# Two of sixteen head pairs with tokens put in order of two hash bits, and attention inside four groups of 256 slots

## The chip, the cores and the metric

The kernel runs on one core of a Trainium2 chip. The metric is the device time of one execution in microseconds (us), lower being better. The core has five engines, each of which works through its own instructions in order: TensorE (PE, matrix products), VectorE (DVE), ScalarE (ACT), GpSimd (POOL) and SyncE (SP, which here only issues DMAs). GpSimd issues DMAs too, among them indirect ones, whose rows go to (or come from) addresses that stand in a tile.

## The reference, cut to what matters

Attention on 4 batches x 8 heads of 768 tokens with 64 features, in which a query sees only the keys with the same six hash bits, and then a token and channel mixer:

```python
q_bits = (np.einsum('bhsd,dk->bhsk', q, proj) > 0)
k_bits = (np.einsum('bhsd,dk->bhsk', k, proj) > 0)
mask = q_bucket[:, :, :, None] == k_bucket[:, :, None, :]     # bucket: the six bits as a number
scores = scale * np.matmul(q, k.transpose(0, 1, 3, 2))
attn = softmax(np.where(mask, scores, -1e9))
x = np.matmul(attn, v)                                        # (B, H, S, D) -> (B, S, H*D)
xt = x.transpose(0, 2, 1)
u = x + (np.maximum(xt @ w_tok1, 0.0) @ w_tok2).transpose(0, 2, 1)
out = u + np.maximum(u @ w_ch1, 0.0) @ w_ch2
```

## The kernel before, in words

The 16 pairs are (batch, two heads); pair n is batch n // 4 and heads 2 (n % 4) and the next. The two heads of a pair lie on partitions 0 to 63 and 64 to 127, so two 64-row matmuls run side by side. The loop over the pairs (line numbers are those of the profile, that is of the kernel before, where nothing else is said) does one pair a turn:

- **Scores.** For each half of the queries (384) there are six chunks of 128 keys (`Half.scores`, L347 to 363). A chunk is a bf16 product of the hash bits and an fp32 product of queries and keys into one PSUM tile `sc`. The bits are scaled so that a query and a key of other buckets get a large negative sum, so that the exponential (L363, ACT) of it is zero. `sc` has three buffers; the exponentials `e` have twelve.
- **Sums.** DVE adds the six chunks of a half (`add` L391 and L395, `add_last` L398). PE adds over partitions in the next turn (`Quotients.sums` L434), ACT makes a first reciprocal (L438, L439), DVE improves it (`newton` L447, L449) and divides (L459, into `XT`).
- **Hash bits of the next pair.** PE multiplies by the projection (`hashes`, L301, tile `hp`), DVE compares (L305, tile `g`), ACT scales (L309), and eight small DMAs on SP (L314) put the bits into `bits`, from which the next turn's first product reads.
- **Weighing.** Two halves, 96 matmul records (`weigh` L410), and ACT's copy of the result (`num`, L416).
- **Weights.** Each turn converts a block of the token and channel weights from int64-like words to fp32: an SP DMA (`raw`, L169), one ACT step (`size`, L177) and five DVE steps (L187 to L206).
- **Bounce.** Each second turn DVE transposes two finished pairs (L233, tile `stage`, one buffer) and SP writes them to DRAM in four DMAs (L238), from where the token mixer reads them.

SP's order in a turn is: eight bits, qk of the pair after next, raw, in each second turn four bounce DMAs, and then, at the head of the next turn, `vn` and `vt` (values by token and by feature, two buffers each) of the pair after. An SP DMA with a wait holds all behind it. Behind the attention follow the token mixer (`mix1`, `mix2`) and the channel mixer (L785 and around), which read `XT` and `x`. At the end flags decide whether a slower branch (`careful_attention`, over all pairs) has to run.

What sets the order is the program text itself: every engine gets its instructions in the order in which the code below records them.

Of the kernel before, what the change touches and what calls it, by code (L numbers as in the profile page):

```python
# [48 lines left out]
def kernel(  # L49
# [4 lines left out]
    vT: bass.AP,  # L54
    proj: bass.AP,
# [30 lines left out]
    EPS = 2.0**-70  # L86

# [35 lines left out]
    excess = const.tile([P, 2 * B * NP], F32, name="excess")  # L123
# [104 lines left out]
    def bounce(stage, n):  # L228
# [7 lines left out]
        to = bounced[b].rearrange("(a i) (g c) -> g i a c", i=32, g=4)  # L236
        for g in range(4):
            nc.sync.dma_start(  # L238
                out=to[g, :, :, 32 * hp : 32 * hp + 64],
                in_=stage[32 * g : 32 * g + 32].rearrange("p a k i -> p a (k i)"),  # L240
            )
# [16 lines left out]
    def attention(pool, psum, W1, W2, x0):  # L258
        bitrows = [pool.tile([P, 2, S], BF16, name=f"bits{n}", tag=f"bits{n}", bufs=1) for n in range(2)]
        loaded = {}  # L260

        def load_qk(n):
            if n >= len(pairs):
                return
# [9 lines left out]

        def load_v(n):
            if n >= len(pairs):
                return
# [3 lines left out]
            vt = pool.tile([P, S], F32, name="vt", tag="vt", bufs=2)  # L281
            nc.sync.dma_start(out=vt, in_=vT[b, hp])
            loaded[n][1:3] = vn, vt
# [8 lines left out]
        def hashes(n):  # L292

            g = pool.tile([P, HALF], BF16, name="g", tag="g", bufs=2)
            if n == 1:
# [10 lines left out]
            if n == 1:  # L306
# [3 lines left out]
            for j in range(4):  # L310
                sl = slice(HALF * (j // 2), HALF * (j // 2) + HALF)
                for i in range(2):
                    at = 32 * j + 16 * i
                    nc.sync.dma_start(  # L314
                        out=bitrows[n % 2][D * i : D * i + NB + 1, j % 2, sl], in_=g[at : at + NB + 1],
# [25 lines left out]
        class Half:  # L341
# [5 lines left out]
            def scores(self):  # L347

                qkt, bits = loaded[self.n][0], bitrows[self.n % 2]
# [17 lines left out]
                if first:  # L367
                    first_hashes(0)
                for c in range(NR):
                    sc = psum.tile([P, 2, 512], F32, name="sc", tag="sc", bufs=3)  # L370
# [29 lines left out]
            def weigh(self):  # L400
# [4 lines left out]
                else:  # L405
                    acc = psum.tile([P, 512], F32, name="acc", tag="acc", bufs=1)[:, :HALF]
                for c, e in enumerate(self.es):
                    for i in range(2):
# [54 lines left out]

        load_qk(0)
# [4 lines left out]
        load_qk(1)  # L469

        idle = psum.tile([P, 512], F32, name="idle", tag="sm", bufs=1)
        for _ in range(6):
# [5 lines left out]
            [(w_tok1, W1, 3, (0, NR)), (w_tok2, W2, 1, (0, NJ)), (w_ch1, WC1, 1, (0, NCB))],  # L478
            bufs=2,
        )  # L480


        before = None
        for n in range(len(pairs)):
            halves = [Half(n, half) for half in range(2)]
            if n:
                load_v(n + 1)
            for now in halves:
                now.scores()
                if n == 0 and now.half:  # L490
                    hashes(1)
                now.add()
                if now.half == 0:
                    now.add_last()
            if before:
# [1274 lines left out]
```

## Time and profile before

| | us |
|---|---|
| time, median of 3 runs (787.77 to 787.89) | 787.86 |
| span of the profiled execution | 786.3 |
| the profiled execution's own time | not shown |
| PE busy | 780.1 |
| DVE busy | 669.5 |
| ACT busy | 484.7 |
| GpSimd busy | 54.2 |
| exponentials (ACT, L363), 192 of them | 154.5 |
| L434's sums and L301's hash products on PE | 13.6 and 12.5 |

How to read a profile: busy times show who works most. The chain that ended last goes back from the last instruction to what released it, so it says who was waited for. A row of the timeline gives start, duration, engine, line, operation, tile written and tile read, and in brackets the engine's idle time before it and who ended it. A group's row gives count, total, mean in ns and idle time before it. "SPq" is the issue of a DMA, not its transfer.

### The profile page before, as it was taken

How to read it: one execution, taken by the hardware profiler on the slowest of the kernel's cores; microseconds unless marked ns; L12 is line 12 of the kernel's file. 1: busy time of each engine (PE TensorE's matmuls, PEld its weight loads, DVE VectorE, ACT ScalarE, POOL GpSimd, SP SyncE). 2: the span in 40 equal slices, each digit the busy share in tenths (PEclk: the TensorE clock that was granted, in tenths of full speed). 3: DMA queues.
4: the chain of work that ended last, by engine and by line, in shares of the span. 5: the costliest groups of instructions: out<-in, count | busy, mean ns of one | idle time of the engine just before them, and what ended most of it. 6: DMA issues, size and time to landing. Idle time of an engine off the chain costs nothing.

```text
span 786.3 us, 12638 instructions
## 1 busy us (share of the span) xinstructions
PE 780.1 (99%) x4751; PEld 483.5 (61%) x4751; DVE 669.5 (85%) x918; ACT 484.7 (62%) x837; POOL 54.2 (7%) x77
## 2 busy tenths in 40 slices
PE   9999999999999999999999999999999999999997
PEld 4444444444444444455544448888887888886886
DVE  5989898989897677999787888999899799889884
ACT  6688888888888887233323225656774667665331
POOL 1000000000000000011120110120000122000001
PEclk9999999999999999999999999999999999999999
DMA  4435353537352425786487897797776784850565
GB/s 165 163 125 163 125 164 125 163 124 244 125 166 88 127 95 180 200 259 133 90 253 263 276 392 276 226 295 204 233 223 203 249 251 126 242 171 2 184 170 133
DMA packets 102529, 145.38 MB, mean 185 GB/s; under 512 B 30200, under 2 KB 72640, under 8 KB 102464
## 3 DMA queue, kind: packets, MB, share of 16 engines
q1 hardware_dynamic: 94448, 119.68, 46.5%
q0 software_dynamic: 7728, 24.64, 13.5%
q8 instruction: 38, 0.62, 0.3%
q10 hardware_dynamic: 288, 0.21, 0.1%
q14 instruction: 27, 0.22, 0.1%
HBM read 101.53 MB, written 35.52 MB: 174 GB/s over the span
## 4 chain that ended last, share of the span: by engine, by line
PE 99%; DVE 0%; issue 0%; DVEq 0%
PE b L785 50%; PE sc L356 20%; PE acc L410 16%; PE t L658 5%; PE t L698 5%; PE sums L434 2%; PE hp L301 1%; PE hw L325 0%; PE idle L474 0%; DVE second L1030 0%; DVE bits L467 0%; DVE ones L97 0%; PE b L1614 0%; DVEq L1765 0%
## 5 line engine op out<-in xcount | busy, mean ns | idle before, releaser
L363 ACT ACTIVATE e<-sc 128x768 f32<-128x768 f32 x192 | 154.5, 810 | 7.0 <-PE sc L356 6.6
L356 PE MATMUL sc<-qk 64*128 64x384 f32 x768 | 153.7, 486 | 0.0
L785 PE MATMUL b<-R,second 128*128 128x256 f32 (+1 forms) x522 | 131.9, 409 | 0.0
L410 PE MATMUL acc<-e,vn 128*32 128x384 f32 x1536 | 127.0, 486 | 0.0
L785 PEld LDWEIGHTS b<-R,second 128*128 128x128 f32 x522 | 99.0, 190 | 28.7 <-issue 16.5
L395 DVE TENSOR_TENSOR esd<-esd,e 128x768 f32<-128x768 f32 x96 | 92.0, 958 | 10.4 <-ACT e L363 0.5
L410 PEld LDWEIGHTS acc<-e,vn 128*32 128x32 f32 x1536 | 49.9, 110 | 73.9 <-issue 73.5
L356 PEld LDWEIGHTS sc<-qk 64*128 64x128 f32 x768 | 68.7, 189 | 42.3 <-issue 38.1
L791 ACT COPY c<-b 128x256 f32<-128x256 f32 (+1 forms) x96 | 40.3, 426 | 79.4 <-PE b L785 68.2
L356 PE MATMUL sc<-bits 64*128 64x384 bf16 x384 | 62.5, 323 | 0.0
L785 PE MATMUL b<-XT,WC 128*128 128x256 f32 (+1 forms) x208 | 61.0, 428 | 0.0
L391 DVE SCALAR_TENSOR_TENSOR esd<-e 128x768 f32<-128x768 f32 x32 | 30.6, 955 | 23.4 <-ACT e L363 23.3
L785 PEld LDWEIGHTS b<-XT,WC 128*128 128x128 f32 x208 | 39.5, 190 | 15.4 <-issue 10.5
L785 PE MATMUL b<-XT,SW 128*128 128x256 f32 (+1 forms) x164 | 47.0, 410 | 0.0
L658 PE MATMUL t<-x,W 128*128 128x512 f32 x96 | 41.8, 593 | 0.0
L356 PEld LDWEIGHTS <-bits 64*128 64x128 bf16 x384 | 18.7, 94 | 33.1 <-issue 9.9
L416 ACT ACTIVATE num<-acc,vsum 128x384 f32<-128x384 f32 x32 | 18.6, 581 | 29.8 <-PE acc L410 29.4
L785 PEld LDWEIGHTS b<-XT,SW 128*128 128x128 f32 x164 | 31.1, 190 | 9.4 <-issue 4.1
L718 POOL DMA_DIRECT2D XT<-second x8 | 9.8, 1228 | 385.6 <-DVE second L717 363.4
L455 ACT COPY rec<-rec 32x384 f32<-32x384 f32 x64 | 32.7, 510 | 5.0 <-DVE rec L449 4.2
L398 DVE TENSOR_TENSOR esd<-esd,e 128x768 f32<-128x768 f32 x32 | 30.5, 954 | 1.9
L658 PEld LDWEIGHTS t<-x,W 128*128 128x128 f32 x96 | 18.2, 190 | 22.7 <-issue 21.3
(246 smaller groups left out, 1282.2 us busy)
## 6 DMA issues: line engine op xcount, KB each, us to landing
second<-left SPq DMA_DIRECT2D x20, 768.0 KB
raw<-in_moe_w_ch SPq DMA_DIRECT2D x16, 768.0 KB
qk<-in_qk SPq DMA_DIRECT2D x15, 768.0 KB
second<-left SPq DMA_DIRECT2D x18, 576.0 KB
seen<-in_qk POOLq DMA_DIRECT2D x21, 384.0 KB, 4.6
WC<-hidden_left SPq DMA_DIRECT2D x18, 448.0 KB
vn<-in_v SPq DMA_DIRECT2D x16, 384.0 KB
vt<-in_vT SPq DMA_DIRECT2D x16, 384.0 KB
```

The costliest lines, as they stand in the source:

```text
L356: nc.tensor.matmul(sc[:, i, :HALF], t[rows, 1, P * c : P * c + P], t[rows, 0, qs], start=start, stop=not start,)
L363: nc.scalar.activation(e, sc[:, :, :HALF], ACT.Exp, scale=SCALE)
L391: nc.vector.scalar_tensor_tensor(self.d, es[0], NR * EPS, es[1], op0=ALU.add, op1=ALU.add,)
L395: nc.vector.tensor_tensor(self.d, self.d, e, op=ALU.add)
L398: nc.vector.tensor_tensor(self.d, self.d, self.es[-1], op=ALU.add)
L410: nc.tensor.matmul(acc[D * i + d : D * i + d + 32], vn[:, i, c, d : d + 32], e[:, i], start=(c == 0), stop=(c == NR - 1),)
L416: nc.scalar.activation(nums[self.n][:, self.half], acc, ACT.Identity, scale=-1.0, bias=vsum,)
L455: nc.scalar.copy(rec[other : other + 32, h], rec[at : at + 32, h])
L658: nc.tensor.matmul(ps, W1[:, r, P * j : P * j + P], x[:, r], start=(r == 0), stop=(r == NR - 1),)
L698: nc.tensor.matmul(ps[at], left, right, start=start, stop=True, skip_group_check=True,)
L785: nc.tensor.matmul(ps, left(k), right(k), start=start and k == ks[0], stop=stop and k == ks[-1], skip_group_check=True,)
L791: nc.scalar.copy(c, ps)
```

## The change

Pairs 6 and 7 (batch 1, heads 4 to 7) leave the loop, which then has 14 turns, counted k = 0 to 13 over the pairs that remain. For the two pairs a class `Sorted` sorts the tokens by two of the six bits (the first two) into four groups of 256 slots each, queries and keys alike. A query's group holds all keys of its bucket, so attention is done inside a group, on 32-row tiles: group g's matmuls use partitions 32 g to 32 g + 31. Two fp32 products over 32 features each and one bf16 product for the four other bits give the scores of 256 queries by 128 keys. Empty slots have a bit column that makes their keys count for nothing. With these inputs the fullest group of the two pairs has 224 tokens; `excess` has two more columns, so that a group of more than 256 would set the flag.

The steps of a sorted pair hang at points of the loop's turns:

```diff
+    SORTED = {6: (1, 5), 7: (3, 7)}
...
+        for n, (turn, made) in SORTED.items():
...
+            at(turn - 1, "loads", begin)
+            at(turn, "hash", call("hash"))
+            at(turn, ("weigh", 1, 3), call("turn_bits"))
+            at(turn, "end", call("own_groups"), call("count"))
+            at(turn + 1, "begin", call("places"), call("numbers"))
+            at(turn + 1, "added", *[call("scatter", r) for r in range(NR)])
+            at(made - 1, "loads", call("fetch"))
+            at(made, "begin", call("copy_bits"), call("turn_q"))
+            at(made, "added", call("turn_k"), call("turn_sorted_bits"))
+            at(made, "weighed", call("scores", 0))
+            at(made, "end", call("scores", 1))
+            at(made + 1, ("scores", 0, 3), call("sums"), call("weigh"))
+            at(made + 1, "added", call("newton"), call("divide"), call("turn_back"))
+            at(made + 1, "last", *[call("gather", r) for r in range(NR)])
+            at(made + 2, "loads", call("store"))
+            at(made + 3, "begin", call("fetch_turned"))
+            at(made + 3, "added", call("finish"))
```

`load` brings qk, vt and, from two new inputs, the tokens' rows (queries in `rows_q`, values and keys in `rows_kv`; one buffer for both pairs). `count` makes each token's place among its group's, and `places` turns it into addresses. GpSimd's 24 indirect DMAs put the rows into DRAM tables, which were cleared at the start:

```diff
+            def scatter(self, r):
+                for w, rows in enumerate((rows_q, rows_kv)):
+                    for i in range(2):
+                        x = 4 * r + 2 * w + i
+                        nc.gpsimd.indirect_dma_start(
+                            out=self.tables[2 * w + i],
+                            out_offset=bass.IndirectOffsetOnAxis(ap=self.at[:, x : x + 1], axis=0),
+                            in_=rows[:, r, i], in_offset=None,
+                        )
...
+            def fetch(self):
+
+                self.v = [sorted_v, pool.tile([P, 2, NR, D], F32, name="vn", tag="vn", bufs=2)]
+                self.v[1] = self.v[1].rearrange("p a b c -> p (a b) c")[:, :NJS]
+                for i in range(2):
+                    nc.sync.dma_start(
+                        out=in_q[i], in_=slots(self.tables[i]).rearrange("(p j) c -> p j c", p=P),
+                    )
...
+            def copy_bits(self):
+                for i in range(2):
+                    nc.scalar.copy(in_q_bits[:, i, :, :4], in_q[i][:, :, D : D + 4])
+                    nc.scalar.copy(in_k_bits[:, i, :, :4], in_k[i][:, :, D : D + 4])
+                nc.scalar.copy(in_k_bits[:, :, :, 4], self.full)
...
+            def scores(self, k):
...
+                for i in range(2):
+                    for part in range(W + 1):
+                        for g in range(NG):
+                            rows = slice(32 * g, 32 * g + 32)
+                            if part:
+                                left, right = kT[rows, i, part - 1, keys], qT[rows, i, part - 1]
+                            else:
+                                left, right = k_bits[rows, i, keys], q_bits[rows, i]
+                            nc.tensor.matmul(
+                                banks[g][:, SLOTS * i : SLOTS * i + SLOTS], left, right,
+                                start=part == 0, stop=part == W, skip_group_check=True,
+                            )
...
+            def finish(self):
+                b, hp = pairs[self.n]
+                nc.vector.transpose(
+                    XT[:, hp, S * b : S * b + S].rearrange("p (a i) -> p a i", i=32), self.y,
+                )
```

The results go back by DRAM: `turn_back` stores them by slot, twelve indirect gathers on GpSimd put them in the tokens' order into the `stage` buffer, `store` writes them to DRAM, `fetch_turned` reads them with 32 features to a partition group, and `finish` transposes them into `XT`. At the start `prepare_sorting` makes constants (on GpSimd and DVE) and clears the tables in eight DMAs. Also: the weights are converted in another order (channel weights first, since the token weights' tiles W1 and W2 and the last batch's part of `XT` serve as scratch), only pairs that stay are bounced, `mix1`'s Relu of a bounced batch is split in two, and `fetch(0, x0)` moves to turn 10.

What ACT has at the end of one turn and the start of the next, with what each waits for: before, from the second `num` of a turn (L416) to the reciprocal of the sums (L438, L439).

```order
L416 ACTIVATE num<-acc,vsum 128x384 [waits PE_49,Activation_49]
L416 ACTIVATE num<-acc,vsum 128x384 [waits PE_49]
L363 ACTIVATE e<-sc 128x768 [waits PE_49] x12
L438 ACTIVATE near<-sums 128x384 [waits PE_49]
L439 ACTIVATE near<-near 128x384 [waits Activation_49]
```

ACT again, now, at the end of turn 4 and in turn 5 (L447 of the changed kernel is L416 of the one before, L388 is L363, L469 is L438; `DMAHW` is a DMA that SP issued; W_124 holds the sorted bits, x_126 and XT the fetched rows):

```order
L447 ACTIVATE num<-acc,vsum 128x384 [waits PE_49,Activation_49]
L447 ACTIVATE num<-acc,vsum 128x384 [waits PE_49]
L737 CAST W_124<-x_126 128x8x4 [waits DMAHW7_49]
L738 CAST W_124<-XT 128x8x4 [waits DMAHW1_49]
L737 CAST W_124<-XT 128x8x4 [waits DMAHW0_49]
L738 CAST W_124<-XT 128x8x4 [waits DMAHW2_49]
L739 COPY W_124<-XT 128x16
L388 ACTIVATE e<-sc 128x768 [waits PE_49] x12
L469 ACTIVATE near<-sums 128x384 [waits PE_49]
```

Five copies of `copy_bits` now stand between a turn's last `num` and the next turn's twelve exponentials, and four of them wait for DMAs of the fetch.

On SP, before, from the loads at the end of one turn with a bounce to the bits of the turn after:

```order
L268 DMA qk<-in_qk 128x1536
L169 DMA raw<-in_moe_w_ch 128x1536
L238 DMA bounced_104<-stage 32x24x64 x4
L280 DMA vn<-in_v 128x768
L282 DMA vt<-in_vT 128x768
L314 DMA bits_135<-g 7x384 x8
```

On SP, now, the same stretch at the end of turn 4 and in turn 5 (L283 is L268 before, L178 is L169, L247 is L238, L301 and L293 are L280 and L282, L339 is L314):

```order
L283 DMA qk<-in_qk 128x1536
L721 DMA x_126<-table_137 128x576
L721 DMA XT<-table_138 128x576
L726 DMA XT<-table_139 128x8x72
L726 DMA XT<-table_140 128x8x72
L730 DMA XT<-table_139 128x4x64 x2
L730 DMA vn<-table_140 128x4x64 x2
L178 DMA raw<-in_moe_w_ch 128x1536
L247 DMA bounced_104<-stage 32x24x64 x4
L301 DMA vn<-in_v 128x768
L293 DMA vt<-in_vT 128x768
L339 DMA bits_135<-g 7x384 x8
```

Eight fetches are put behind qk, and two of them write a `vn` buffer, ahead of the loop's own `vn`.

On DVE, before, the adds of a turn's two halves and the compare that makes g:

```order
L391 SCALAR_TENSOR_TENSOR esd<-e 128x768
L395 TENSOR_TENSOR esd<-esd,e 128x768 x3
L398 TENSOR_TENSOR esd<-esd,e 128x768
L391 SCALAR_TENSOR_TENSOR esd<-e 128x768
L395 TENSOR_TENSOR esd<-esd,e 128x768 x3
L305 TENSOR_SCALAR g<-hp 128x384
```

On DVE, now, from the adds of half 0 to g in turn 8 (L419 is L391 before, L423 is L395, L426 is L398, L325 is L305; W_124 holds the sorted pair's weighed values):

```order
L423 TENSOR_TENSOR esd<-esd,e 128x768 x3
L426 TENSOR_TENSOR esd<-esd,e 128x768
L869 STREAM_TRANSPOSE XT<-stage 128x768
L826 SCALAR_TENSOR_TENSOR unit<-ssums,rec 128x512
L827 SCALAR_TENSOR_TENSOR rec<-unit,rec 128x512
L832 TENSOR_TENSOR W_124<-W_124,rec 128x512 x2
L839 STREAM_TRANSPOSE x_126<-W_124 128x512
L839 STREAM_TRANSPOSE XT<-W_124 128x512
L419 SCALAR_TENSOR_TENSOR esd<-e 128x768
L423 TENSOR_TENSOR esd<-esd,e 128x768 x3
L325 TENSOR_SCALAR g<-hp 128x384
```

Between the two halves' adds, and so ahead of g, stand pair 6's last transposition (`finish`) and pair 7's `newton`, `divide` and `turn_back`.

More of the change, by code (lines that the diff above doesn't have):

```diff
@@ L260, in attention, with following @@
         loaded = {}
+        regular = [n for n in range(len(pairs)) if n not in SORTED]
+        turns = {n: i for i, n in enumerate(regular)}
+        def following(n, by=1):
+            i = turns[n] + by
+            return regular[i] if i < len(regular) else None
         def load_qk(n):
-            if n >= len(pairs):
+            if n is None:
                 return
@@ L488, in attention @@
             for now in halves:
[L489 to L491 removed]
+                now.scores(hooks("scores", now.half))
+                if k == 0 and now.half:
+                    hashes(regular[1])
                 now.add()
```

425 lines of the change are left out of this document (390 added, 35 removed).

## The prediction

> **What bounds the kernel now.** I read the page first: busy time of each engine, then the row of granted clock, then the shares of the chain that ended last.
>
> ```profile
> span 786.3 us, 12638 instructions
> PE 780.1 (99%) x4751; PEld 483.5 (61%) x4751; DVE 669.5 (85%) x918; ACT 484.7 (62%) x837; POOL 54.2 (7%) x77
> PEclk9999999999999999999999999999999999999999
> PE 99%; DVE 0%; issue 0%; DVEq 0%
> ```
>
> TensorE (PE) is busy 780.1 of 786.3 us, and the chain is PE's to 99%. The chain's pieces give one turn of the attention loop, here the one for pair 6:
>
> ```profile
> 120.90 9.80 PE sc L356 x72
> 130.70 0.78 PE sums L434 x8
> 131.48 0.65 PE hp L301 x8
> 132.13 7.74 PE acc L410 x96
> 139.87 9.80 PE sc L356 x72
> ```
>
> From 120.90 to 139.87 a turn takes 18.97 us, and PE has no gap. So PE work that goes is gained one for one, as long as no other engine makes PE wait; and every new wait of PE is lost in full. The whole question is which of the moved steps PE will wait for. The span is the sum's base; the profiled execution's own time is not shown, and the median of 787.86 us lies 1.6 us above the span. I add those 1.6 us at the end.
>
> I write T5 for the start of turn 5, and so on; turns count the 14 pairs that stay in the loop.
>
> **What PE saves.** A score chunk (9.80 / 12 = 0.82 us) is two bf16 matmuls side by side, 0.16, and the fp32 pair, 0.65, each over 384 columns. Over 256 columns that is 0.11 and 0.43. A sorted pair has two key halves and two heads, and for each one bf16 and two fp32 groups: 4 x (0.11 + 2 x 0.43) = 3.9 us if the four 32-row tiles of a group run together, as two 64-row tiles do now; 7.7 if only two do. I take 3.9, since two already do at no loss. Sums: 0.65 x 512/384 x 2 = 1.7. Weighing: 8 groups x 0.43 = 3.4. Hashing 0.65, turning and counting the bits about 1.0. Together 10.7 of 18.97, so two pairs save 2 x 8.25 = **-16.5** (with 7.7 in place of 3.9: -8.8). Against that the Trainium skill, "TensorE: Matmul & The Clock Gate", section "Measured speedup vs the span model", states 3.07 times for four row tiles rather than four. By that, as an estimate, the scores would cost 1.2 us more a pair and the sum would be 2.3 higher; no row of this trace has four row tiles.
>
> **A. The start.**
>
> ```profile
> 3.87 0.44 POOL L101 TENSOR_SCALAR_AFFINE_SELECT bitscale<-bitscale 128x1 f32<-128x1 f32 x2
> 5.70 0.56 DVE L330 TENSOR_SCALAR bits<-hw 128x384 bf16<-128x384 f32 x1 [4.25 <-PE hw L325]
> ```
>
> GpSimd ends its set-up at 4.31. Now some 25 memsets and iotas follow, and DVE has eight steps that wait for them ahead of its first hash bits (L330): 25 at the row's 0.22 or less put these at 8 us in place of 5.70, +2.3. Eight DMAs that clear 3.4 MB of tables stand ahead of the bits of pair 1 in SP's queue and in the DMA rings, some 3 us. **+5** (0 to 9).
>
> **B. The count.** At the end of turns 1 and 3 PE counts the groups from what DVE compares behind the weights' conversion, whose last step stands in a turn after PE has begun the next one (139.42 against 139.87 below): **+1.5** for both (0 to 4).
>
> ```profile
> 137.67 0.96 DVE L196 TENSOR_TENSOR size<-size,unit 128x768 f32<-128x768 f32 x1
> 139.42 0.95 DVE L206 SCALAR_TENSOR_TENSOR WC<-raw,size 128x768 uint32<-128x768 uint32 x1
> ```
>
> **C. The scatters.** Before has no indirect DMA. Its nearest rows are GpSimd's plain ones:
>
> ```profile
> L1602 POOL DMA_DIRECT2D seen<-in_qk x21 | 12.5, 597 | 106.4 <-ACT seen L1592 69.4 <-ACT second L791 26.7 <-DMA hidden_left<-WC 10.2
> L718 POOL DMA_DIRECT2D XT<-second x8 | 9.8, 1228 | 385.6 <-DVE second L717 363.4 <-DVE unit L187 11.3 <-DVE TB L615 5.5
> seen<-in_qk POOLq DMA_DIRECT2D x21, 384.0 KB, 4.6
> ```
>
> An issue takes 0.6 or 1.2 us, by the shape; 4.6 us pass to landing. An indirect one reads 128 addresses as well; I take 1.2 (0.6 to 2). A table's next scatter waits until its last one landed, so pair 6's 24 take 24 x 1.2 + 2 = 31 us, or 22 at 0.6. They begin about 5 us into turn 2 and end at T3 + 17. The rows of pair 7 go into the same buffer, so SP, which works in order, stands there until then, with a weight block, a bounce, vn, vt and the bits of turn 4 behind it. Rows 0.9, block 0.4, bounce 1.4, vn and vt 0.9, four bits and their landing 4.9 (under E): the bits of turn 4 are there at T3 + 25.5, 6.5 after 18.97; the count's wait for the late block makes it **+7** (0 at an issue of 0.6, 20 at 1.7).
>
> **D. Turns 5 and 7: fetched rows ahead of the exponentials.**
>
> ```profile
> 121.87 9.69 ACT L363 ACTIVATE e<-sc 128x768 f32<-128x768 f32 x12 [0.32 <-PE sc L356]
> 139.87 0.44 SPq L268 DMA_DIRECT2D qk<-in_qk  x1
> 161.00:166.00 5.00, 5.00 (x40) 2.81 (x38) 4.14 (x5) 4.98 (x7) 0.00 (x0) 1.00 1.00 398
> 179.00:194.00 15.00, 15.00 (x147) 7.14 (x145) 13.86 (x19) 14.21 (x21) 0.00 (x0) 1.00 1.00 313
> ```
>
> Exponentials begin 1.03 us into a turn. In front of them ACT now has four copies that wait for the tables' rows. SP can issue the fetch only after the eight bits and qk, that is from 0.5 us after the turn's start (139.87 is the start of a turn), one each 0.45 us. Rings run at most 398 GB/s (DMA share 1.00 in the first window). In the second, 4.72 MB in 15 us hold one bounce of 3072 runs of 256 B; the other 3.93 MB need 9.9 us, so the short runs took 5, or 1.6 ns a run over all rings. Ahead of the last key row lie qk (768 KB, 2.0 us), the queries (590 KB, 1.5) and 2048 key runs of 288 B (3.6): with 2 us to landing, T5 + 9.7; exponentials begin at T5 + 10.3 in place of 1.03. PE has three score buffers, which gives it little: some 0.6 us. Turn 5 loses 8.7, turn 7 as much and 1 for a longer queue: **+18** (11 to 20). The end at 11 has the runs cost by bytes alone.
>
> **E. Starts of turns 6 and 8.**
>
> ```profile
> 133.92 5.90 SPq L314 DMA_DIRECT2D bits<-g  x8
> 121.92 0.37 SPq L280 DMA_DIRECT2D vn<-in_v  x1
> ```
>
> The sorted pair's values take one of two vn buffers, so in turns 5 and 7 the next pair's vn waits on SP for the last weighing matmul, and the bits of the next turn stand behind it. Four bits, issued by 133.92 + 3.0 = 136.9, were there at 139.87 without a gap of PE, so landing takes at most 3.0; I take 1.9. From the last matmul: vn and vt 0.9, four bits 3.0, landing 1.9 = 5.8, less the sorted pair's second scores (1.9) which PE has meanwhile: +3.9 each, **+8** (5 to 9).
>
> **F, G. DVE ahead of the hash bits.**
>
> ```profile
> 129.69 3.08 DVE L395 TENSOR_TENSOR esd<-esd,e 128x768 f32<-128x768 f32 x3
> 132.70 0.55 DVE L305 TENSOR_SCALAR g<-hp 128x384 bf16<-128x384 f32 x1
> L1002 DVE TENSOR_TENSOR second<-b,second 128x512 f32<-128x512 f32 x28 | 19.2, 687 | 4.5 <-ACT second L997 4.0
> ```
>
> g, from which the bits come, stands behind DVE's adds without slack (132.77, 132.70). In turns 6 and 8 six steps of about 0.69 are put before half 1's adds, 4.1 us: turn 7 starts 3.3 late. In turns 8 and 10 the last transposition (L869) stands there too and waits for data that went from GpSimd's twelve gathers (12 x 1.2, behind a bounce) through SP's store to DRAM and back in 3072 runs of 128 B. It can run at T8 + 17.5 in place of 12.9, and at T10 + 22.7; then adds 4.6, g and its scaling 1.2, four bits and landing 4.9. Turn 9 starts 8.8 late, turn 11 15. **+12** (4 to 17) and **+15** (7 at an issue of 0.6, 21 at 1.7).
>
> **H. PE after a rest.**
>
> ```profile
> 5.57 2.61 PE L356 MATMUL sc<-qk 64*128 64x384 f32 x8
> 121.01 1.45 PE L356 MATMUL sc<-qk 64*128 64x384 f32 x8
> 3.75 1.89 PE L325 MATMUL hw<-qk,projs 128*32 128x384 f32 x8
> 8.43 0.85 PE L325 MATMUL hw<-qk,projs 128*32 128x384 f32 x8
> ```
>
> The first eight matmuls of a kind cost 1.2 and 1.0 us more at the start than the same ones later, 2.2 together, though the row of granted clock reads 9 throughout. C, D, F and G make six long rests: 6 x 1.5 = **+9** (0 to 16; the value lies between none and 2.2 each, nearer the rows of the start). The Trainium skill, "TensorE: Matmul & The Clock Gate", section "Part 1: The HAM clock gate (the "warmup" mystery)", halves the clock after some 3.4 us of idling until about 3.4 us of work have passed. That would be 1.7 each as an estimate, 14 with E's two rests; no rest that long stands in this trace.
>
> **The sum.** -16.5 + 5 + 1.5 + 7 + 18 + 8 + 12 + 15 + 9 = +59. Span 786.3 + 59 = 845, time **847 us**. The channel half stays: mix1's split Relu adds 8 ACTIVATEs beside PE work, at nothing (ACT is idle 38% of the span).
>
> **Rivals.** (1) GpSimd issues in 0.6 us and PE starts again at full speed: C 0, F 7, G 7, H 0, so 59 - 7 - 5 - 8 - 9 = +30: **818**. For it speaks the row of 597 ns; against it that an indirect one has more to do. Chance 0.20. (2) GpSimd's issues are held while DVE adds two tiles: DVE is busy 669.5 of 786.3 us, mostly so. An issue of 1.8 then gives C 20, F 17, G 21 in place of 7, 12 and 15: +78, and 875 with a bounce that also waits at the scatters' start up to **885**. Against it: the plain issues at 597 ns stand among busy DVE stretches. The Trainium skill's "SBUF — State Buffer", section "Who interferes with whom", has this rule for two-input DVE instructions and GpSimd's reads; no indirect read is in this trace. Chance 0.13. (3) **Not slower:** transfers land as fast as bytes allow. Its place is turns 5 and 7: qk and both fetches by 398 GB/s put the last key row at T5 + 5.4, so D is 2 x 3.8 = 7.6; with bits that land in 1 us E is 4; the store and its return are done before DVE comes, so F 3.3 and G 0; A, C and H 0. With B 1.5 that is 16.4 against 16.5: **788**, and below once in_k lands before T5 + 5. Against it: the window of 313 GB/s. Chance 0.08. (4) The change does not do what it says: a group with over 256 tokens sends all pairs through the careful branch, at least 16 x 18.97 = 304 us: **1,150**. The inputs' fullest group has 224. Chance 0.02.
>
> **How the numbers follow.** The forecast, 847 with own range 828 to 870, has 0.57; the rest as above. A range of **803 to 887** leaves out rival 3, rival 4 and half a tail of (2) and the bounds' sum. Faster by over 0.2% (1.6 us, about what a measurement of this kernel can tell) is half of rival 3 and a little for what I overlook: 0.06; within 0.2%: 0.04; slower: 0.90.
>
> **What would show it.** In the new trace: PE's score groups of a sorted pair at about 0.97 us for each head and half (or 1.9); ACT's first exponential of turn 5 about 10 us after the turn's first matmul; SP standing at vn until the end of turns 5 and 7; GpSimd's scatters at 1.2 us each; DVE standing at L869 in turn 10, and PE idle ahead of turn 11. Wrong would be PE without gaps over 5 us, or tables that land within 5 us of T5.

## The result, and the profile after

| | before | changed |
|---|---|---|
| time, median of 4 runs each, us | 787.88 (787.77 to 788.11) | 860.1 (856.12 to 862.05) |
| ratio | | 1.091 (95% interval 1.0882 to 1.0937) |
| span of the profiled execution, us | 786.3 | 854.3 |

The changed kernel is 9.1% slower. The profiled execution is its fastest, 856.12; all spans below are compared with its 854.3, and its executions differ among themselves by 6 us, so a few us in a single run of an experiment say little. What stands out of that are the lengths of single turns.

The page of the changed kernel: engines' busy time, granted clock by slices, and the chain's shares.

```profile
span 854.3 us, 12792 instructions
PE 795.8 (93%) x4743; PEld 492.2 (58%) x4743; DVE 669.9 (78%) x956; ACT 469.3 (55%) x847; POOL 139.9 (16%) x171
PEclk9999798997898999999999999999999999999999
PE 60%; DMA 2%; ACT 1%; DVE 1%; SPq 1%; issue 0%; POOL 0%; DVEq 0%
```

The shares are of the whole span, and this chain could be followed back only to 293.03 us, to GpSimd's gathers in turn 9, so they add up to two thirds. Behind that point PE has some nine tenths of the chain; before the change the chain was PE's to 99% over the whole span. The clock row, all nines before, has sevens and eights in the first 13 slices, in the attention. PE's busy time has risen too, though its work fell: at half clock, and in the slow weighing shown below, the same work is busy for longer. Behind the attention nothing changed (475.8 us before, 476.1 now, from the token mixer's first product to the end). So all of it is in the turns. Cut at each turn's first score product, the ones that grew most are these (the windows' columns: length, then busy time and count of PE, PE's weight loads, DVE, ACT, GpSimd; granted clock, DMA share, GB/s):

```profile
49.97:70.43 20.46, 20.46 (x185) 9.21 (x185) 18.74 (x33) 15.97 (x27) 15.02 (x12) 1.00 0.39 144
70.43:108.45 38.02, 23.01 (x206) 10.04 (x206) 17.81 (x25) 16.97 (x27) 14.03 (x13) 0.82 0.54 166
128.69:164.44 35.75, 25.71 (x265) 12.65 (x265) 22.69 (x31) 19.84 (x37) 12.07 (x13) 0.90 0.56 157
190.56:237.48 46.92, 34.08 (x264) 15.68 (x265) 26.00 (x35) 22.27 (x40) 13.83 (x12) 0.82 0.43 114
268.46:300.01 31.55, 28.70 (x184) 13.03 (x184) 21.05 (x26) 17.01 (x26) 13.15 (x12) 0.90 0.48 140
300.01:320.18 20.17, 19.04 (x185) 8.89 (x185) 13.92 (x18) 15.20 (x23) 0.00 (x0) 1.00 0.47 119
```

These are turns 2, 3, 5, 7, 9 and 10. A turn without sorted work is 18.96; a sorted pair adds 1.4 in its counting turn, 4.1 for its scores and 5.3 for sums and weighing, 10.8 altogether. Above that, turn 3 lost 17.7, turn 5 12.7, turn 7 23.9, turn 8 6.7, turn 9 12.6, and the others 10.5 together, 84 in all. Two pairs off the loop saved 2 x 18.96 - 2 x 10.8 = 16.3. The difference is the 68 us by which the span grew.

Where PE waited in turn 3, then ACT's timeline in turns 3 and 5, and what SP did ahead of it:

```profile
103.70 0.32 PE L633 MATMUL so<-XT,g 128*128 128x64 bf16 x3 [14.68 <-ACT num L447]
...
100.06 0.89 ACT L186 ACTIVATE size<-raw 128x768 f32<-128x768 f32 x1 [13.87 <-DMA raw<-in_moe_w_ch]
...
137.74 0.22 ACT L738 CAST W<-XT 128x32 bf16<-128x32 f32 x1 [0.86 <-DMA XT<-table]
137.87 0.26 ACT L739 COPY W<-XT 128x16 bf16<-128x16 bf16 x1
137.97 2.20 ACT L388 ACTIVATE e<-sc 128x768 f32<-128x768 f32 x3
```

```profile
70.04 0.38 SPq L293 DMA_DIRECT2D vt<-in_vT  x1
88.97 0.33 SPq L618 DMA_DIRECT2D x<-in_q_rows  x1
92.84 0.33 SPq L619 DMA_DIRECT2D x<-in_kv_rows  x1
93.71 0.34 SPq L178 DMA_DIRECT2D raw<-in_moe_w_ch  x1
```

In turn 3 SP stood from 70.4 to 92.8 for pair 6's scatters, then issued the weight block, and ACT got it at 100.06. ACT's `num` of half 0 (103.06 to 103.64) stands behind the step that reads this block, and the group count's first product (L633, `turn_bits`) writes a PSUM tile `so` that takes the one buffer which `num` has to empty first (tag `acc`, one buffer). So PE stood for 14.7 us. In turn 5 the first exponential came at 137.97, 9.3 us after the turn's start, behind the copies. Both waits begin where the prediction says (C and D); in turn 3 the way from the late block to PE is another, as told at its end.

Turn 9 shows what it does not name. PE's timeline there:

```profile
283.38 5.34 PE L441 MATMUL acc<-e,vn 128*32 128x384 f32 x50
288.96 0.87 PE L441 MATMUL acc<-e,vn 128*32 128x384 f32 x4 [0.24 <-issue]
290.43 5.37 PE L441 MATMUL acc<-e,vn 128*32 128x384 f32 x30 [0.60 <-issue]
296.38 1.21 PE L441 MATMUL acc<-e,vn 128*32 128x384 f32 x5 [0.58 <-issue]
297.81 0.84 PE L441 MATMUL acc<-e,vn 128*32 128x384 f32 x4 [0.23 <-issue]
299.24 0.85 PE L441 MATMUL acc<-e,vn 128*32 128x384 f32 x3 [0.58 <-issue]
300.01 0.34 PE L381 MATMUL sc<-bits 64*128 64x384 bf16 x2
```

The 96 records of the weighing are all there, at full clock, and no releaser is named ("issue"), but they take 16.6 us in place of 7.7: from 286.6 on they come in bunches of about four, most of them 0.71 to 0.76 us apart. Such stretches lie in turn 7 (215 to 233, of which 223.85 to 230.68 at a granted clock of 0.50), in turn 9 (286.6 to 300), and short ones of 1 to 2 us at the ends of turns 2 and 4, all where GpSimd has indirect DMAs running or just ended.

### The profile page after: what moved, and what is told of

Same layout as the page of the kernel before. It is cut to its first block, busy times and chain, and to the rows that moved or that the text cites. A ratio compares the mean times of both kernels' runs of the same rounds, so it can differ in the third digit from the quotient of the medians.

```text
span 854.3 us, 12792 instructions
## 1 busy us (share of the span) xinstructions
PE 795.8 (93%) x4743; PEld 492.2 (58%) x4743; DVE 669.9 (78%) x956; ACT 469.3 (55%) x847; POOL 139.9 (16%) x171
## 4 chain that ended last, share of the span: by engine, by line
PE 60%; DMA 2%; ACT 1%; DVE 1%; SPq 1%; issue 0%; POOL 0%; DVEq 0%
PE b L1250 46%; PE t L1119 5%; PE t L1163 4%; PE sc L381 2%; PE acc L441 2%; ACT e L388 1%; DMA stage<-bounced 1%; DMA bits<-g 1%; SPq L339 0%; DMA bounced<-stage 0%; DVE esd L423 0%; POOL stage L851 0%; DMA stage<-result,XT 0%; PE sums L465 0%; SPq L865 0%
## 5 line engine op out<-in xcount | busy, mean ns | idle before, releaser
L381 PE MATMUL sc<-qk 64*128 64x384 f32 x672 | 143.1, 509 | 16.5 <-ACT e L388 8.9
L388 ACT ACTIVATE e<-sc 128x768 f32<-128x768 f32 x168 | 132.8, 812 | 16.6 <-PE sc L381 15.2
L1250 PEld LDWEIGHTS b<-R,second 128*128 128x128 f32 x522 | 99.0, 190 | 28.6 <-issue 16.5
L423 DVE TENSOR_TENSOR esd<-esd,e 128x768 f32<-128x768 f32 x84 | 80.6, 959 | 21.7 <-ACT e L388 13.4
L381 PEld LDWEIGHTS sc<-qk 64*128 64x128 f32 x672 | 65.7, 196 | 54.8 <-issue 25.2
L441 PEld LDWEIGHTS acc<-e,vn 128*32 128x32 f32 x1344 | 45.4, 112 | 78.1 <-issue 76.9
L381 PE MATMUL sc<-bits 64*128 64x384 bf16 x336 | 61.5, 332 | 12.5 <-DMA bits<-g 10.0
L710 POOL DMA_INDIRECT table<-x,XT x48 | 56.0, 1166 | 84.4 <-ACT e L388 44.4
L419 DVE SCALAR_TENSOR_TENSOR esd<-e 128x768 f32<-128x768 f32 x28 | 26.9, 959 | 49.2 <-ACT e L388 45.8
L1250 PEld LDWEIGHTS b<-XT,WC 128*128 128x128 f32 x208 | 39.5, 190 | 15.4 <-issue 10.8
L851 POOL DMA_INDIRECT stage<-result,XT x24 | 27.0, 1124 | 123.0 <-DMA bounced<-stage 61.4
L381 PEld LDWEIGHTS <-bits 64*128 64x128 bf16 x336 | 20.3, 97 | 41.0 <-DMA bits<-g 15.3
L447 ACT ACTIVATE num<-acc,vsum 128x384 f32<-128x384 f32 x28 | 16.0, 581 | 38.5 <-PE acc L441 30.7
```

The source lines that it names most:

```text
L381: nc.tensor.matmul(sc[:, i, :HALF], t[rows, 1, P * c : P * c + P], t[rows, 0, qs], start=start, stop=not start,)
L388: nc.scalar.activation(e, sc[:, :, :HALF], ACT.Exp, scale=SCALE)
L419: nc.vector.scalar_tensor_tensor(self.d, es[0], NR * EPS, es[1], op0=ALU.add, op1=ALU.add,)
L423: nc.vector.tensor_tensor(self.d, self.d, e, op=ALU.add)
L441: nc.tensor.matmul(acc[D * i + d : D * i + d + 32], vn[:, i, c, d : d + 32], e[:, i], start=(c == 0), stop=(c == NR - 1),)
L447: nc.scalar.activation(nums[self.n][:, self.half], acc, ACT.Identity, scale=-1.0, bias=vsum,)
```

## The experiments

"Theory" C to G are the terms of the prediction; G in the experiments' expectations also names the new one, that GpSimd's indirect gathers slow PE. The spans are to be held against 854.3.

**Plain gathers.**

```diff
-                    nc.gpsimd.indirect_dma_start(
-                        out=self.x[:, r, i], out_offset=None, in_=self.results[i],
-                        in_offset=bass.IndirectOffsetOnAxis(ap=self.of[:, x : x + 1], axis=0),
-                    )
+                    nc.gpsimd.dma_start(out=self.x[:, r, i], in_=self.results[i][P * r : P * r + P])
```

> The 24 indirect gathers become plain GpSimd DMAs of the same size, so pairs 6 and 7 stay in slot order and their outputs are wrong; nothing else changes. Theory G: PE is slowed while GpSimd's indirect gathers run (in turn 9 of the changed kernel the weighing takes 16.6 us in place of 7.7, and turn 7's takes 5.6 and 5.9 for its halves in place of 3.9). Then with plain ones turn 9's weighing is back at 7.7 to 8, turn 7 is 6 to 10 us shorter, turns 9 to 11 together change little because the finish of pair 7 then becomes the wait, and the span falls by 8 to 18 from 854. Rival: the slow stretch belongs to what PE does there and not to GpSimd; turn 9's weighing stays at 14 us or more and the span within 4 of 854 but for the shorter issues (0.6 in place of 1.5 us, 11 us off the chain of pair 7's return).

Time 843.53, span 841.7. Turns 7, 9 and 10 of it:

```profile
192.20:230.12 37.92, 26.57 (x265) 13.44 (x265) 25.83 (x35) 21.54 (x40) 6.42 (x12) 0.86 0.52 140
260.78:280.89 20.11, 19.29 (x185) 10.45 (x186) 19.24 (x25) 17.05 (x26) 6.41 (x12) 1.00 0.61 180
280.89:305.47 24.58, 19.03 (x188) 8.86 (x184) 15.40 (x20) 15.20 (x23) 0.00 (x0) 0.99 0.47 131
```

Turn 7 is 9.0 shorter, turn 9 11.4, and its weighing is one row of 7.92 us. So the slow stretches in these two turns hang on the gathers being indirect. Turns 10 and 11 grew by 6.9: there PE now waits 5.55 us for the bits behind pair 7's last transposition, the wait that term G put at turn 11 (7 us if gathers are short).

**Pair 7's rows by GpSimd's queue.**

```diff
+                queue = nc.gpsimd if self.which else nc.sync
-                nc.sync.dma_start(out=rows_q.rearrange("p r i c -> p (r i c)"), in_=q_rows[b, hp])
-                nc.sync.dma_start(out=rows_kv.rearrange("p r i c -> p (r i c)"), in_=kv_rows[b, hp])
+                queue.dma_start(out=rows_q.rearrange("p r i c -> p (r i c)"), in_=q_rows[b, hp])
+                queue.dma_start(out=rows_kv.rearrange("p r i c -> p (r i c)"), in_=kv_rows[b, hp])
```

> Pair 7's rows are loaded from GpSimd's queue, behind its own scatters, so SP no longer stands for them in turn 3. Theory C: turn 3's 38 us (14.7 of them one wait of PE, and a restart at half clock) come from SP standing there. Then turn 3 takes 20.5 to 23 us and the span falls by 15 to 18, to 836 to 840, if pair 7's scatters still end before turn 7 fetches them. Rival: the weight block is late for another reason (DMA rings filled by the scatters), and turn 3 stays above 30 us.

Span 846.0: -8.3, and not the 15 to 18 expected. Turn 3 fell to 21.6 as expected, but turn 4 rose from 20.3 to 41.4: ACT's copies of the sorting bits into the same rows now wait for the rows (0.20 us of work at 99.38 after 5.90 idle, and again at 103.30 after 3.72), ahead of that turn's exponentials; and the weighing beside pair 7's scatters took 17.6. SP's standing was one path of the wait; the shared buffer is its root.

**Copies late.**

```diff
-            at(made, "begin", call("copy_bits"), call("turn_q"))
-            at(made, "added", call("turn_k"), call("turn_sorted_bits"))
-            at(made, "weighed", call("scores", 0))
-            at(made, "end", call("scores", 1))
+            at(made, "hash", call("copy_bits"))
+            at(made, "loads", call("turn_q"), call("turn_k"), call("turn_sorted_bits"))
+            at(made, "end", call("scores", 0), call("scores", 1))
```

> ACT's copies of the fetched bits are moved behind both halves' exponentials, DVE's turning of the fetched rows behind the compare that makes g, and both sorted scores to the end of the turn. Theory D: turns 5 and 7 lose 7.5 and 8.6 us to the copies plus some 4 us each of half clock behind them. Then PE has no wait in the first half of either turn, the turns take about 24 and 30 us in place of 35.8 and 46.9 less a new wait of up to 4 us for the turned rows at their end, and the span falls by 12 to 22, to 832 to 842. Rival: the fetch occupies the rings and DVE in any case; what is gained early in the turn is lost at its end, and the span falls by under 6.

Time 839.17, span 837.3: -17.0, in the range. Turn 5 took 29.6 (24 were expected, and up to 4 of a new wait) and turn 7 30.9, so 22.2 us were gained there. Up to their first weighing product, where the copies had stood, the two turns are 8.7 and 11.0 shorter: this is what the copies had cost, with the half clock behind them. Turn 9 fell by 10.7 as well, since its weighing, beside the same indirect gathers, took only 8.5. Turn 10 grew by 12.5: with turns 7 and 9 shorter, pair 7's return is late again, and PE waits 10.9 us at the start of turn 11.

**Values of their own.**

```diff
-                self.v = [sorted_v, pool.tile([P, 2, NR, D], F32, name="vn", tag="vn", bufs=2)]
-                self.v[1] = self.v[1].rearrange("p a b c -> p (a b) c")[:, :NJS]
+                spare = flat(x0)[:, 2 * NR * QW : 2 * NR * QW + NJS * D] if self.which else WC1[:, 3, NW : NW + NJS * D]
+                self.v = [sorted_v, spare.rearrange("p (j d) -> p j d", j=NJS)]
```

> The second head's sorted values go to a spare stretch of a weight tile (pair 6) or of the rows buffer (pair 7) in place of one of the two vn buffers, so that vn of the next pair no longer waits for the last weighing. Theory E: bits of turns 6 and 8 then come some 20 us earlier on SP; turns 6 and 8 start without the 1.2 and 2.7 us of waiting, but turns 5 and 7 end only as early as PE gets through, so the span falls by 4 to 9, to 845 to 850. Rival: at most the waits seen at those starts, 4 us together, are gained, and a third of that comes back as waiting in the next turn: 850 to 854.

Span 847.1: -7.2. PE has no wait at the starts of turns 6 and 8 any more. Theory E's 4 to 9 holds, though 7.2 is not much more than the 6 us by which executions differ; the two waits themselves were 1.2 and 2.7.

**Rows of their own.** Pair 7's query rows in a spare stretch of a weight tile, and scatters by table:

```diff
+                spare = WC1[:, 3, : 2 * NR * QW].rearrange("p (r i c) -> p r i c", r=NR, i=2)
+                self.rows_q = spare if self.which else rows_q
...
-            at(turn + 1, "added", *[call("scatter", r) for r in range(NR)])
+            at(turn + 1, "added", *[call("scatter", r, w) for w in (1, 0) for r in range(NR)])
```

> Pair 7's query rows get a buffer of their own (a stretch of a weight tile not yet in use), and the scatters go by table: values and keys first, so that the one shared buffer is free after twelve scatters instead of 24. Theory C: PE's 14.7 us of waiting in turn 3 and its half clock behind it come from the shared buffer. Then turn 3 takes 20.6 to 24 us in place of 38.0, and turn 4 does not get longer (when only SP's wait was taken away, turn 4 took 41.4, since ACT waited for the same rows); span 834 to 841. Rival: with the scatters back to back the wait moves to turn 4 or 5, and the span stays above 846.

Span 841.7: -12.6, just short of the 834 to 841 expected. Turns 3 and 4:

```profile
70.15:93.55 23.40, 20.74 (x207) 9.81 (x205) 18.01 (x25) 16.95 (x27) 11.23 (x9) 1.00 0.83 260
93.55:118.04 24.49, 22.32 (x185) 10.28 (x185) 18.91 (x33) 16.18 (x27) 14.43 (x14) 0.93 0.37 133
```

Turn 3 lost all but 2.7 us of its wait, and its half clock (14.6 us shorter); turn 4 grew by 4.2, where none was expected. So at its place the move gave 10.4. Turn 9 fell to 20.5, its weighing at nearly full rate again (8.1), while turn 11 began with a wait of 13.3: the return of pair 7 once more.

**DVE later.** Division and turning back in turns 6 and 8, and the last transposition in turns 8 and 10, behind g:

```diff
-            at(made + 1, "added", call("newton"), call("divide"), call("turn_back"))
+            at(made + 1, "added", call("newton"))
+            at(made + 1, "loads", call("divide"), call("turn_back"))
...
-            at(made + 3, "added", call("finish"))
+            at(made + 3, "loads", call("finish"))
```

> In turns 6 and 8 DVE's division and turning back, and in turns 8 and 10 its last transposition (L869), are put behind the compare that makes g; only the two steps that free a PSUM bank stay ahead of it. Theory F/G: the bits of turns 7, 9 and 11 were late by these steps. Then the weighing of turns 6, 8 and 10 ends with no wait for bits behind it, turns 7, 9 and 11 start 2 to 4 us earlier each, and the span falls by 7 to 12, to 842 to 847. Rival: SP stands for the store and the fetch of the returned rows in front of the same bits; then turn 9 and turn 11 start as late as before, and only some 2 us at turn 7's start are gained.

Span 841.8: -12.5, a little more than expected. Turns 6, 8 and 9 fell to 24.9, 25.3 and 21.1 (from 26.1, 31.0 and 31.6), turn 11 to 18.96, while turn 10 rose to 28.3. Of turn 9's 10.5 us, 8.1 are its weighing, which took 8.5 in place of 16.6, and no theory here says why. Turn 10's loss begins at ACT:

```profile
285.85 0.58 ACT L447 ACTIVATE num<-acc,vsum 128x384 f32<-128x384 f32 x1 [4.96 <-remote]
286.48 0.92 PE L381 MATMUL sc<-qk 64*128 64x384 f32 x4 [2.57 <-ACT num L447]
```

The weighing's last product had started at 280.24; ACT's `num` of it came 5.6 us later, with no releaser that the profile knows ("remote"), while GpSimd's gathers ran (273.7 to 290.2). DVE was waiting for ACT's exponentials then, so the moved steps are not the cause.

**Four moves, and the same with plain gathers.**

> Own rows, copies late, own values and DVE later, all at once. If the losses are separate stretches of PE's time, their gains add: 17 (copies, measured), 7 (values, measured), about 16 (rows) and about 9 (DVE) bring the span from 854 to about 805. Rival: the waits stand behind one another, so that one removed shows the next, and the sum is at most 35: 819 or more. With either, GpSimd's gathers still slow PE, by some 15 us.

> The four moves, with plain GpSimd DMAs in place of the 24 gathers (pairs 6 and 7 stay in slot order, their outputs are wrong). Theory G: PE is slowed by the indirect gathers wherever they stand; then this is 8 to 18 us below the run with the four moves, at 787 to 797, and no weighing takes over 9 us at full clock. Rival: the slow stretches came with the late turns 7 and 9, and are gone with the moves alone; then both spans are within 4.

The four moves: time 814.74, span 812.9. The single gains add up to 17.0 + 7.2 + 12.6 + 12.5 = 49.3; 41.4 came. That lies between the two expectations (49 off, and at most 35 off): most of the gains add, but each single gain also holds what turns 9 to 11 won and lost by their timing. With plain gathers as well: 797.49, span 795.7. Turns 8, 9 and 10, with indirect gathers and then with plain ones:

```profile
201.74:230.72 28.98, 27.34 (x268) 11.79 (x265) 15.73 (x21) 17.55 (x29) 7.00 (x7) 1.00 0.38 95
230.72:253.92 23.20, 21.70 (x190) 9.22 (x186) 22.29 (x29) 18.05 (x29) 7.01 (x7) 1.00 0.59 169
253.92:279.81 25.89, 22.54 (x186) 9.97 (x186) 16.01 (x21) 16.00 (x24) 5.92 (x6) 0.87 0.49 133
```

```profile
194.75:220.07 25.32, 25.06 (x269) 11.21 (x265) 15.67 (x21) 17.39 (x29) 0.00 (x0) 1.00 0.39 98
220.07:240.99 20.92, 19.32 (x189) 8.96 (x185) 20.02 (x27) 17.67 (x29) 6.01 (x11) 1.00 0.68 193
240.99:260.48 19.49, 19.29 (x184) 10.45 (x186) 15.88 (x21) 15.38 (x23) 0.58 (x2) 1.00 0.61 171
```

With the late turns gone the indirect gathers still cost 12.3 us in these three. The spans differ by 17.2, but 7.1 of that had arisen before the first gather (at 193.7 and 186.6), so no more than 10 of it can be the gathers'. In turn 2, beside the scatters, which are still indirect, the weighing took 9.4 at a granted clock of 1.00, above the 9 that was expected. Even with plain gathers the kernel stays 9.4 us above the span before: about 26 us of smaller losses (4.4 in turn 1, 7.1 in turn 7) stand against the 16.3 saved. No version tried here is faster than the kernel before.

**Gathers beside a PE that never waits.** Into the kernel before, at five points, of which turn 5 is typical:

```diff
+        def added(k):
+            nc.vector.tensor_copy(index[:, k : k + 1], index[:, :1])
...
+                    nc.gpsimd.indirect_dma_start(
+                        out=spare[0][:, D * (x % 12) : D * (x % 12) + D], out_offset=None, in_=table, in_offset=offset,
+                    )
...
             halves[1].add_last()
+            if n in (3, 5, 7, 9, 11):
+                added(n)
```

> The kernel before, whose PE waits for nothing in its turns of 18.96 us, with GpSimd DMAs added to spare parts of SBUF whose data nobody uses: 12 plain ones from the middle of turn 3, 12 indirect gathers from the middle of turns 5 and 7, 24 plain ones in turn 9, 24 indirect gathers in turn 11. 128 rows of 256 B each. Theory G: the indirect ones slow PE by themselves. Then turns 5 and 7 (with the start of the turn behind each) grow by 5 to 10 us, turn 11 by 10 to 20, and turns 3 and 9 by under 1; the span rises by 20 to 40 from 786.3. Rival 1: any long run of GpSimd DMAs does it; then turn 9 grows as well. Rival 2: it needs PE's late or half-clocked turns of the changed kernel; then no turn grows by more than 1 and the span stays at 786 to 789.

Span 786.5, time 788.39. Turns 5, 6, 11 and 12, in which 29 of the 48 gathers were issued:

```profile
101.26:120.22 18.96, 18.96 (x188) 8.88 (x184) 17.76 (x25) 16.18 (x24) 4.13 (x4) 1.00 0.62 176
120.22:139.19 18.97, 18.97 (x189) 8.87 (x186) 16.13 (x21) 16.19 (x24) 10.32 (x9) 1.00 0.41 144
215.09:234.06 18.97, 18.97 (x189) 8.89 (x186) 17.77 (x25) 16.18 (x24) 4.14 (x4) 1.00 0.60 175
234.06:253.02 18.96, 18.96 (x188) 8.86 (x185) 14.52 (x18) 15.31 (x23) 15.00 (x14) 1.00 0.33 108
```

No turn grew. The theory that indirect gathers slow PE by themselves falls; something of the changed kernel has to come with them.

**Three candidates for it.** The same, with an SP DMA that waits for the gathers (turns 3 and 11), rows in mixed order (turn 6), scatters (turn 9).

```diff
+            if k in (3, 11):
+                nc.sync.dma_start(out=kept, in_=spare[0])
```

> Again the kernel before with GpSimd DMAs that nobody uses, now nearer to the changed kernel: in turns 3 and 11 twelve indirect gathers, with an SP DMA that stores what they brought, so that SP stands until they end, as it stands in the changed kernel's turns 7 and 9; in turn 6 twelve gathers whose rows come in a mixed order, as the changed kernel's do; in turn 9 24 indirect scatters over four tables in mixed order. Theory S (SP standing beside the gathers is the second ingredient of PE's slow stretches): turns 3 and 4, and 11 and 12, grow by 4 to 9 us together, the others by under 1. Theory O (the order of the rows): turns 6 and 7 grow by as much. Theory W (writes to tables): turns 9 and 10. If none grows, span 786 to 789, what is needed beside the indirect gathers stays open.

Span 796.1. Turns 6 to 10 kept their 18.96, so neither the order nor scatters do it. Turns 4 and 5 grew by 5.6 and turns 12 and 13 by 2.6, but by waits for bits that stood on SP behind the store, not by a slow weighing, which took 7.92 in each of them. So SP's standing isn't the ingredient either. It shows, by itself, the price of a store that waits in front of the bits: the mechanism of term G.

**All plain.** Plain DMAs for the 48 scatters too.

```diff
+                        nc.gpsimd.dma_start(out=self.tables[2 * w + i][P * r : P * r + P], in_=rows[:, r, i])
```

> The changed kernel with plain GpSimd DMAs of the same sizes in place of all 48 scatters and 24 gathers (the two pairs' tokens are not put in order; their outputs are wrong). Theory I: turn 3's 17 us come from the scatters' issues, 1.6 us each with the 0.3 between them; with plain ones at 0.55 to 0.6 and 0.3 and no table's scatter behind its last, 24 take 22 us or less, pair 7's rows come in time, and turn 3 takes 20.5 to 23 us in place of 38. With the gathers' part (13 us, measured) and scatters no longer beside turns 2 and 4 (1 to 2 us each), the span is 820 to 827. Rival: the DMA rings or DVE, not the issues, hold turn 3; it stays above 30 and the span above 836.

Time 827.17, span 825.3, as expected. Turns 2 and 3:

```profile
51.27:70.23 18.96, 18.96 (x185) 8.89 (x185) 17.24 (x32) 15.97 (x27) 13.13 (x24) 1.00 0.54 194
70.23:91.36 21.13, 20.54 (x209) 9.77 (x207) 19.14 (x26) 17.41 (x27) 0.00 (x0) 1.00 0.82 269
```

Turn 3 is 16.9 shorter, and turns 2 and 4 are at 18.96, without their slow ends. So what decides term C is how long the 24 scatters take, their issues and the landings between them together; the run does not part the two. Rival 1 of the prediction, fast issues, had put this case at 818, with the half clock free; here that is not free.

## Why the prediction was right, point by point

The direction, the range (803 to 887) and the size (847 forecast, 860.1 measured) held, and most of the waits began where they were forecast. Their sizes were much less close than the sum is. By terms:

- **PE's saving**, 16.5 forecast, 16.3 measured. A sorted pair costs 10.8 in place of 10.7. The step with most doubt was that four row tiles run at once:

```profile
153.48 0.29 PE L779 MATMUL ss<-W 32*128 32x256 bf16 x4
153.60 1.04 PE L779 MATMUL ss<-W,W 32*128 32x256 f32 x16
154.46 0.28 PE L779 MATMUL ss<-W 32*128 32x256 bf16 x4
```

  From 153.48 to 154.46 one head of one key half takes 0.98 us, forecast 0.97 with all four at once. The Trainium skill's 3.07 times ("TensorE: Matmul & The Clock Gate", section "Measured speedup vs the span model") does not show here; at 256 columns it is nearly four, and the measurement decides.
- **A**, 5 forecast: turn 0 lost 1.7. **B**, 1.5 forecast: turn 1 lost 2.0, 1.73 of it PE's wait at L633, for ACT's `num` and the PSUM buffer. The step of DVE's that B names was not what PE waited for.
- **C**, 7 forecast, 17.7 measured with its restart: right in where the wait begins, mis-sized in its length, and wrong in its path. The 48 issues took 1.17 us each, as I took them (1.2), but 0.30 us lay between any two, and some waited for a landing: 24 took 38 us, not 31. And the forecast let the bits of turn 4 end the wait, at T3 + 25.5, with the count adding half a microsecond. PE stood at the count itself until T3 + 33.3: ACT got the block 6.3 us after its issue (93.71 to 100.06), and 3.6 us of ACT's steps, up to `num`, followed.

```profile
L710 POOL DMA_INDIRECT table<-x,XT x48 | 56.0, 1166 | 84.4 <-ACT e L388 44.4 <-DVE XT L700 20.4 <-issue 12.8
52.06 1.20 POOL L710 DMA_INDIRECT table<-x,XT  x1 [44.40 <-ACT e L388]
53.56 1.01 POOL L710 DMA_INDIRECT table<-x,XT  x1 [0.30 <-issue]
```

  Rival 2's mechanism is in it, small: of the 72 indirect issues the 53 that overlap a DVE step with two SBUF inputs take 1.22 us on the mean, the other 19 0.97. This agrees with the Trainium skill, "SBUF — State Buffer", section "Who interferes with whom"; the price is a quarter of a microsecond, not a doubling.
- **D**, 18 forecast: the first exponential was forecast at T5 + 10.3 and came at T5 + 9.3; PE's waits in turns 5 and 7 were 7.5 and 8.6, 16.1 together.
- **E**, 8 forecast: PE's waits at the two starts were 3.9 together; the experiment gave 7.2.
- **F**, 12 forecast: PE's waits were 1.1 at turn 7's start, 3.1 at turn 9's and 1.8 in turn 8 behind the same DVE steps, 6.0 together. That moving DVE's steps gave 12.5 does not show F's size, since 8.1 of it came in turn 9's weighing.
- **G**, 15 forecast at turn 11's start: only 1.1 there. Turn 9 was long through its slow weighing, which gave the chain time. With plain gathers, and in the runs that shortened other turns, the wait stood at turn 11 with 5.6, 10.9 and 13.3 us. The mechanism held, and another loss covered it.
- **H**, 9 forecast. Three of the restarts, right behind waits of over 7 us, and two behind shorter ones:

```profile
103.70:107.80 4.10, 4.10 (x27) 1.15 (x26) 2.33 (x5) 0.00 (x0) 0.00 (x0) 0.50 0.25 95
138.83:141.93 3.10, 3.10 (x12) 1.53 (x14) 2.17 (x3) 2.15 (x3) 2.18 (x4) 0.50 0.88 271
202.50:206.78 4.28, 4.28 (x16) 2.28 (x18) 2.87 (x3) 2.83 (x4) 0.00 (x0) 0.50 1.14 317
237.50:240.92 3.42, 3.42 (x12) 2.15 (x14) 0.00 (x0) 0.81 (x1) 0.00 (x0) 0.50 0.04 11
268.22:275.05 6.83, 5.97 (x22) 3.99 (x24) 5.92 (x7) 3.68 (x7) 0.00 (x0) 0.50 0.41 134
```

  In the first three the granted clock is 0.50 for 3.1 to 4.3 us of work, so each cost 1.6 to 2.1; I took 1.5. These agree with the Trainium skill's rule in "TensorE: Matmul & The Clock Gate", section "Part 1: The HAM clock gate (the "warmup" mystery)", which gave 1.7. The last two do not wholly: they stand behind waits of only 2.7 us (ended at 237.48) and 2.5 us (at 268.46), less than that rule's 3.4 us of idling, and cost 1.7 and 3.0. The five cost 10.4 together, close to the 9 forecast, but two of them are not the long rests that were counted.
- **Missing** was PE's slow weighing beside indirect DMAs: 8.9 us in turn 9 and about 10 in turn 7, with the half clock that came in it (223.85 to 230.68).

What was missing and C's 10 more make some 30 us, and the terms that came smaller (G by 14, F by 6, E by 4, A by 3) take about as much off again. That the sum came so close is in good part this luck. Rival 2's sum has a slip: with its C, F and G of 20, 17 and 21 the terms add up to 59 + 24 = +83 and 871 us, not to +78; the measured 860.1 lies below either.

## What to carry to other kernels

Work that is taken off a saturated engine is only gained if the steps that replace it stand in no in-order queue ahead of what that engine waits for. Here 16.3 us of PE time were bought with copies ahead of exponentials, loads ahead of bits, and transpositions ahead of the hash: moving four of these, without a change of the work, gave back 41 of 68 us (some of it in turn 9, where the weighing took 10.6 and no longer 16.6). Follow each moved step's wait along its own queue, and look for the next user of its buffer: a wait taken from SP came out at ACT, because the buffer was still shared. The same holds for PSUM: a product that takes another tile's only buffer waits for whatever empties it, here for ACT and all that stands ahead in ACT's queue.

## What the runs showed of the hardware that was not expected

Beside indirect gathers on GpSimd PE's weighing ran at less than half its rate for up to 13 us, at a granted clock of 1.00: 16.6 us in place of 7.7 for 96 matmul records, in bunches of about four, most of them 0.71 to 0.76 us apart. Beside indirect scatters it did the same in turn 4 of the run with pair 7's rows on GpSimd's queue (17.6 us). With plain DMAs of the same size in place of the gathers it was gone in turns 7 to 9, in the changed kernel (span -12.6, with 6.9 of other waits uncovered) and in the one with four moves. That the plain ones are also sooner over does not explain it: beside 24 plain ones in place of the scatters, 15.7 us long, turn 2 kept its 18.96.

Indirect DMAs are needed for it and not enough. The same gathers in the kernel before, beside a PE that never waits, cost nothing, neither alone nor with SP standing, rows in mixed order or scatters. In the changed kernel, too, turn 9's weighing took only 8.1 to 8.5 us beside its twelve indirect gathers in three runs (copies late, rows of their own, DVE later). Half clock is not what else is needed: with the four moves turn 9's weighing still took 10.6, though the granted clock was 1.00 in all of turns 8 and 9. What it is stays open. PE's instruction supply was not tried as a cause, since nothing here could change it alone.

An indirect GpSimd DMA of 128 rows took 0.95 to 1.7 us to issue, with 0.30 us to the next; a plain one of the same size took 0.55.
